# Batch 0's q of the first chunk loaded in 2-KB rows and turned by products with a 64-column selector

## The chip, the core and the metric

The kernel runs on one core of a Trainium2 chip. The metric is the device time of one execution in microseconds (us), the median over several runs. Engines: TensorE (PE, with its weight loads as PEld), VectorE (DVE), ScalarE (ACT), GpSimd (POOL), and SyncE (SP), which only issues DMAs.

## What is computed

Attention with a decay per head in blocks of 64 tokens, for 4 batches, 8 heads, 768 tokens and head dimension 64, and behind it a two-layer network with 512 inputs and 2048 hidden units. All inputs and the output are fp32.

```
for b in range(S // 64):
    qb, kb, vb = q[:, :, sl], k[:, :, sl], v[:, :, sl]
    intra = (qb @ kb.T * Dmask) @ vb              # Dmask[i, j] = lam**(i-j) for i >= j, else 0
    inter = (qb * lam**(pos+1)) @ kv_state
    out[:, :, sl] = intra + inter
    kv_state = lam**64 * kv_state + (kb * lam**(63-pos)).T @ vb
x = out, as (4*768, 512)
h = x @ w_in
g = h + sin(alpha*h)**2 / alpha
result = g @ w_out
```

## The kernel before

**Chunks.** The tokens go in six chunks of 128 per batch (`T = 128`, `NT = 6`); one chunk of all four batches makes a group of 512 tokens for the network. The code is written out by hand in the order in which each engine shall run it (`manual_schedule`): each engine executes its own instructions in that order, and semaphores join them. While the network of group g runs (`hidden`, `project`), the attention of the next chunk is woven in between.

**First chunk.** It has its own path, since nothing runs beside it. Per batch: k and q are turned so that the head dimension lies on partitions (`turn`, `turn_in_two`, `turn_rows_begin` and `turn_rows_end`), `scores1` makes the scores of all eight heads in two PSUM banks and VectorE multiplies them by the mask table `C0` into `STm` (L356), and `outs` multiplies by v and brings the result, for all but batch 0 with the factor table `Etab` (L370), into `xt`, the input of `hidden`. In batch 0 the factor lam**(i+1) is already in q, so `outs(0, 0, 6, A)` copies without a factor.

**Loads.** k and q of batch 0 come as fp32 through SP's hardware queue (`raw_k`, `raw_q`, L81), in rows of one token and head (64 numbers, 256 bytes); everything else comes through GpSimd's software queue, in this order: k and q of batches 1 to 3 (L104, L114), v of all batches (L104, L125), `w_in` in five pieces (L89), `w_out`'s first block (L92), and then the next chunk. GpSimd's loads convert to bf16 on the way.

**Rows of eight tokens.** q of batches 1 to 3 is loaded by `load_q_rows` with eight tokens of one head on one partition (2 KB a row), partition p holding head p % 8 and tokens 8 (p // 8) to 8 (p // 8) + 7. `turn_rows` turns this with sixteen products per batch: for each of the eight places e in a row, and each half of the heads, 64 columns of q against 64 columns of `by_head`, a permuted identity. They write fp32 in PSUM; L314 copies to `QKT`.

**Batch 0's q.** `raw_q` has one token per partition and all heads. VectorE multiplies it by `Rq` (128 x 8: factor by token and head, an exponential on ScalarE at L179 of `lnlam` with the column `pcol[:, 1]`) into bf16 (L578). `turn_in_two` makes four 128 x 128 transposes (L295), and ScalarE and VectorE copy half each (L296, L297).

**Small tables.** GpSimd's iota makes `dist` (column less partition). From it VectorE makes `iden`, the columns of `pcol` (L149), the triangle `tri` (L155), `tri64` (two 64 x 64 copies, L158, read only by the `mask_table` of the later chunks), `pos_row` (L163), `idf` (L164) and, once `lnlam` is there, `ln_x` (L186) and `by_head` (L188). `spin` puts products on TensorE whose result nobody reads.

Of the kernel before, what the change touches and what calls it, by code (L numbers as in the profile page):

```python
# [15 lines left out]
def kernel(  # L16
# [11 lines left out]
    nc = tc.nc  # L28
    P = nc.NUM_PARTITIONS

    B, H, S, D = q.shape
    T = 128
    NT = S // T
    HP = H // 2
# [23 lines left out]
    def bank(nm, n, dtype=FP32):  # L58
        return psum.tile([P, 512 if dtype is FP32 else 1024], dtype, name=nm, tag=f"b{n}")
# [16 lines left out]
            d[t] = p.tile([P, B, H, D], BF16, name=nm)  # L76

    raw = {}
    for nm, eng in (("k0", nc.sync), ("q0", nc.sync)):
        raw[nm] = rawp.tile([P, H, D], FP32, name=f"raw_{nm}")  # L80
        eng.dma_start(out=raw[nm][:], in_=NAT[nm[0]][1][int(nm[1]), :, 0:T, :].rearrange("h p e -> p h e"))  # L81
# [23 lines left out]

    new_chunk(0)
    new_chunk(1)
    E8 = T * H // P

    def q_rows(b):  # L110
        return qn[0][:, b].rearrange("p h d -> p (h d)")

    def load_q_rows(b):
        nc.gpsimd.dma_start(out=q_rows(b), in_=q[b, :, 0:T, :].rearrange("h (n e) d -> n h (e d)", e=E8))  # L114
# [21 lines left out]
    def spin(n, bk, cols=256):  # L136
        ps = bank("hps", bk)
        for _ in range(n):
            nc.tensor.matmul(out=ps[:, 0:cols], lhsT=fill[:, 0:P], rhs=fill[:, 0:cols], start=True, stop=True)  # L139
# [3 lines left out]
    pcol = consts.tile([P, 5], FP32, name="pcol")  # L143
# [4 lines left out]
    def column(rows, n, factor, base):  # L148
        nc.vector.tensor_scalar(out=pcol[rows, n:n + 1], in0=dist[rows, 0:1], scalar1=factor, scalar2=base,  # L149
                                op0=ALU.mult, op1=ALU.add)  # L150
# [3 lines left out]
    column(ALL, 0, 1.0, -1.0)  # L154
    nc.vector.tensor_scalar(out=tri[:], in0=dist[:], scalar1=0.0, scalar2=None, op0=ALU.is_ge)  # L155
    tri64 = consts.tile([P, D], FP32, name="tri64")
    for half in HALF:
        nc.vector.tensor_copy(out=tri64[half, :], in_=tri[half, half])  # L158
    column(ALL, 2, 1.0, T - 1.0)
    for n, half in enumerate(HALF):  # L160
        column(half, 3, 1.0, n * D - 1.0)
        column(half, 4, 1.0, (n + 1) * D - 1.0)
    nc.vector.tensor_scalar(out=pos_row[:], in0=dist[:], scalar1=pcol[:, 1:2], scalar2=None, op0=ALU.add)  # L163
    nc.vector.tensor_scalar(out=idf[:], in0=dist[0:NFC, 0:NFC], scalar1=0.0, scalar2=None, op0=ALU.is_equal)  # L164
# [12 lines left out]
    def powers(nm, n, src, shape):  # L177
        t = consts.tile(shape, FP32, name=nm)
        nc.scalar.activation(out=t[:], in_=src, func=ACTF.Exp, scale=pcol[:, n:n + 1])  # L179
        return t  # L180

    Rq = powers("Rq", 1, lnlam[:, 0:H], [P, H])
    NE = powers("NE", 0, by_pair, [P, 2, HP])
    ln_x = consts.tile([P, NDC], FP32, name="ln_x")
    for hd, half in enumerate(HALF):
# [19 lines left out]
    def decay_of_pair(pr):  # L205
        for hd, half in enumerate(HALF):
            nc.scalar.activation(out=L64[half, pr, :], in_=lnlam[half, pr + hd:pr + hd + H - 1:2],
                                 func=ACTF.Exp, scale=float(D))
# [80 lines left out]
        else:  # L289
            nc.scalar.copy(out=both[t][:, :, b, :, :], in_=ps)  # L290

    def turn_in_two(t, b, n):
        ps = bank("T_ps", n, BF16)[:].rearrange("p (n c i) -> p n c i", n=2, c=HP)[:, 1]
        for hp in range(HP):
            nc.tensor.transpose(out=ps[:, hp, :], in_=qn[t][:, b, 2 * hp:2 * hp + 2, :], identity=iden[:])  # L295
        nc.scalar.copy(out=both[t][:, 1, b, 0:2, :], in_=ps[:, 0:2])  # L296
        nc.vector.tensor_copy(out=both[t][:, 1, b, 2:4, :], in_=ps[:, 2:4])  # L297

    rows_ps = {}

    def turn_rows(b, es):
# [276 lines left out]
    nc.vector.tensor_tensor(out=qn[0][:, 0, :, :], in0=raw["q0"][:], op=ALU.mult,  # L578
                            in1=Rq[:].unsqueeze(2).broadcast_to([P, H, D]))
# [234 lines left out]
```

## Time and profile before

| what | value |
|---|---|
| median of 3 runs | 207.41 us (207.37 to 207.46) |
| the profiled execution | 207.33 us |
| its span, from the first instruction to the last | 205.6 us |
| granted TensorE clock, mean | 0.999 |
| TensorE busy | 198.1 us, 96% of the span |
| VectorE, ScalarE, GpSimd busy | 131.5, 143.2 and 106.5 us |
| software DMA queue | 74528 packets, 13.37 MB |

The span is what the profile's times refer to, from 0; the 1.7 us between span and time lie around it. A row of the timeline gives start, length, engine, line, operation, what is written from what, its shape, how many were merged into the row, and in brackets the idle time of the engine before it with what ended it. A stretch of the windows view gives for each engine busy time and number of instructions, then the granted clock, the mean load of the 16 DMA engines and the GB/s that they moved (bytes written).

### The profile page before, as it was taken

What the parts mean: (1) busy time and instruction counts of PE and PEld (TensorE: products, weight loads), DVE (VectorE), ACT (ScalarE), POOL (GpSimd) and SP (SyncE); (2) the same over time, 40 slices, a digit from 0 to 9 for tenths busy, and PEclk for the clock granted to TensorE, in tenths of its full rate; (3) what the DMA queues carried; (4) which work ended last, traced back from release to release, by engine and by line L of the source; (5) the groups of instructions that cost most, each with busy time, mean ns of one, the idle gap of its engine ahead of it and who ended that gap; (6) DMA issues with size and microseconds to landing.
All of it is one profiled execution on the core that took longest, in us unless ns stands there. A gap on an engine that the chain in (4) does not pass through costs nothing.

```text
span 205.6 us, 5385 instructions
## 1 busy us (share of the span) xinstructions
PE 198.1 (96%) x2235; PEld 98.3 (48%) x2265; DVE 131.5 (64%) x219; ACT 143.2 (70%) x241; POOL 106.5 (52%) x112
## 2 busy tenths in 40 slices
PE   7999989999999999999999999999999999999994
PEld 2764445554454444445444445444445444444443
DVE  7794979473889878967556967555967544444000
ACT  7798987224999799676776666776666787887121
POOL 8999939988979975999966930002000000000000
PEclk9999999999999999999999999999999999999999
DMA  8999999999989999899999929401101101110213
GB/s 132 170 178 205 203 162 176 189 176 154 150 275 105 128 151 184 82 150 155 152 149 155 181 64 192 117 3 51 54 0 54 51 0 54 53 51 0 104 51 105
DMA packets 96683, 24.49 MB, mean 119 GB/s; under 512 B 87938, under 2 KB 94226, under 8 KB 96658
## 3 DMA queue, kind: packets, MB, share of 16 engines
q0 software_dynamic: 74528, 13.37, 86.9%
q1 hardware_dynamic: 22128, 10.76, 25.5%
q8 instruction: 18, 0.29, 0.6%
q14 instruction: 7, 0.06, 0.1%
q10 hardware_dynamic: 2, 0.00, 0.0%
HBM read 27.27 MB, written 6.29 MB: 163 GB/s over the span
## 4 chain that ended last, share of the span: by engine, by line
PE 84%; DMA 7%; POOL 6%; issue 1%; ACT 1%; POOLq 0%; ACTq 0%
PE ops L535 39%; PE hps L507 35%; DMA w_out<-in_moe_w_out_dram 7%; PE O_ps L457 2%; POOL w_in L89 2%; PE hps L560 2%; PE F_ps L443 2%; PE KV_ps L423 2%; POOL kn L104 1%; PE O_ps L482 1%; POOL vn L104 1%; PE T_ps L338 1%; POOL qn L114 1%; POOL vn L125 1%; ACT QKT L344 1%
## 5 line engine op out<-in xcount | busy, mean ns | idle before, releaser
L524 DVE SCALAR_TENSOR_TENSOR gall<-s,r_sb,hps 128x512 bf16<-128x512 bf16 x96 | 71.1, 745 | 44.5 <-ACT s L515 44.3
L507 PE MATMUL hps<-xt,w_in 128*128 128x512 bf16 x369 | 94.3, 379 | 1.1 <-issue 0.3
L535 PE MATMUL ops<-w_out,gall 128*128 128x512 bf16 x353 | 90.4, 380 | 1.7 <-DMA w_out<-in_moe_w_out_dram 0.6
L510 ACT ACTIVATE s_sb<-hps,alpha_sb 128x512 bf16<-128x512 f32 x96 | 65.2, 684 | 32.0 <-PE hps L507 31.5
L515 ACT ACTIVATE s<-s_sb 128x512 bf16<-128x512 bf16 x91 | 57.3, 630 | 2.8
L507 PEld LDWEIGHTS <-w_in 128*128 128x128 bf16 x384 | 36.6, 98 | 42.8 <-DMA w_in<-in_moe_w_in_dram 0.3
L535 PEld LDWEIGHTS <-gall 128*128 128x128 bf16 x368 | 34.6, 98 | 41.5 <-DMA w_out<-in_moe_w_out_dram 1.1
L257 POOL TENSOR_TENSOR kdec<-kn,R 128x1024 bf16<-128x1024 bf16 x12 | 22.9, 1937 | 4.2 <-DMA kn<-in_k_dram 4.1
L392 POOL CAST sb<-S 128x512 bf16<-128x512 f32 x20 | 12.3, 621 | 21.3 <-DVE S L399 21.3
L388 POOL TENSOR_TENSOR SD<-S,L 128x512 f32<-128x512 f32 x16 | 16.8, 1050 | 8.6 <-DVE S L399 8.5
L489 DVE TENSOR_TENSOR xt<-O_ps,Etab 128x512 bf16<-128x512 f32 x20 | 12.8, 684 | 6.4 <-PE O_ps L482 6.4
L104 POOL DMA_DIRECT2D vn<-in_v_dram x13 | 14.7, 1137 | 0.0
L542 DVE COPY o_sb<-ops 128x512 f32<-128x512 f32 x15 | 10.3, 689 | 4.2 <-PE ops L535 4.2
L450 DVE TENSOR_TENSOR STm<-F_ps,C 128x512 bf16<-128x512 f32 x20 | 12.8, 683 | 0.3 <-PE F_ps L443 0.3
L544 ACT COPY o_sb<-ops 128x512 f32<-128x512 f32 x8 | 4.6, 576 | 12.0 <-PE ops L535 12.0
L399 DVE TENSOR_TENSOR S<-SD,KV_ps 128x512 f32<-128x512 f32 x16 | 10.8, 683 | 0.1
L104 POOL DMA_DIRECT2D kn<-in_k_dram x9 | 10.0, 1113 | 0.4 <-issue 0.3
L344 ACT COPY QKT<-T_ps 128x512 bf16<-128x512 bf16 x8 | 4.3, 586 | 5.3 <-PE T_ps L341 5.3
L139 PE MATMUL hps<-fill 128*128 128x256 bf16 (+1 forms) x24 | 6.5, 391 | 1.4 <-DVE fill L132 1.4
L104 POOL DMA_DIRECT2D qn<-in_q_dram x6 | 7.1, 1188 | 0.0
L457 PEld LDWEIGHTS <-sb 64*64 64x64 bf16 x320 | 4.3, 108 | 4.8 <-issue 4.7
L356 DVE TENSOR_TENSOR STm<-F_ps,C 128x512 bf16<-128x512 f32 x8 | 5.2, 686 | 0.8 <-PE F_ps L352 0.4
(92 smaller groups left out, 116.8 us busy)
## 6 DMA issues: line engine op xcount, KB each, us to landing
out_dram<-o_sb SPq DMA_DIRECT2D x19, 256.0 KB, 2.4
vn<-in_v_dram POOLq DMA_DIRECT2D x10, 256.0 KB, 7.9
w_out<-in_moe_w_out_dram POOLq DMA_DIRECT2D x4, 512.0 KB, 10.8
w_in<-in_moe_w_in_dram POOLq DMA_DIRECT2D x3, 512.0 KB, 9.4
kn<-in_k_dram POOLq DMA_DIRECT2D x6, 256.0 KB, 8.7
qn<-in_q_dram POOLq DMA_DIRECT2D x6, 256.0 KB, 8.5
out_dram<-o_sb SPq DMA_DIRECT2D x8, 128.0 KB, 1.8
kn<-in_k_dram POOLq DMA_DIRECT2D x4, 240.0 KB, 6.7
```

The source lines that it names most:

```text
L104: nc.gpsimd.dma_start(out=to, in_=by_head)
L257: nc.gpsimd.tensor_tensor(out=kdec[t][:, b0:b1, :, :], in0=kn[t][:, b0:b1, :, :], in1=R[:, o:o + H].unsqueeze(1).unsqueeze(3).broadcast_to ...
L388: nc.gpsimd.tensor_tensor(out=pair(SD, pr), in0=pair(S_of[n], pr), op=ALU.mult, in1=L64[:, pr].unsqueeze(1).unsqueeze(3).broadcast_to([P, ...
L392: nc.gpsimd.tensor_copy(out=pair(dst, pr), in_=pair(S_of[n], pr))
L399: nc.vector.tensor_tensor(out=S, in0=pair(SD, pr), in1=ps, op=ALU.add)
L450: nc.vector.tensor_tensor(out=st[:, hd], in0=att["F", t, pr, hd], op=ALU.mult, in1=of_mask(C64, t, pr, hd).unsqueeze(1).broadcast_to([P, 2 ...
L489: nc.vector.tensor_tensor(out=xview(t)[:, 2 * pr:2 * pr + 2, blk, :, :], in0=att["O", t, pr, blk], in1=Eb, op=ALU.mult)
L507: nc.tensor.matmul(out=hps[:], lhsT=w[:, c, (f % 4) * P:(f % 4 + 1) * P], rhs=xt[g][:, c, :], start=(c == 0), stop=(c == NDC - 1))
L510: nc.scalar.activation(out=s_sb[:], in_=hps[:], func=ACTF.Sin, scale=alpha_sb[:, f:f + 1])
L515: nc.scalar.activation(out=s2[:], in_=s_sb[:], func=ACTF.Square)
L524: nc.vector.scalar_tensor_tensor(out=gall[g][:, f, :], in0=s2[:], scalar=r_sb[:, f:f + 1], in1=hps[:], op0=ALU.mult, op1=ALU.add)
L535: nc.tensor.matmul(out=ops[:], lhsT=gall[g][:, f, m * P:(m + 1) * P], rhs=w_out_sb[part][:, f % 4, :], start=(f == 0), stop=(f == NFC - 1))
```

## The change

Batch 0's q is loaded in the same rows of eight tokens as the other batches, still as fp32 through SP's queue. Its factor is therefore no longer by token (partition) and head (column), but by head and token group (partition) and place in the row (column): `Rq` is now the exponential of `pos8`, the token's number plus one, scaled by a column `ln_row` that holds the logarithm of the partition's own head. To make these, seven small VectorE operations are new: `of_head` (which head a partition has, a sum over `iden`), `by_number`, two columns of `pcol`, `pos8`, `ln_h` and `ln_row`. The product with `Rq` goes ahead of the first mask table. Batch 0 is turned by sixteen products like the others, `turn_in_two` is dropped, and the two copies by halves now read fp32. The two fill products (`spin(2, 3)`) are dropped. The first half of batch 1's row products goes behind batch 0's scores. The copies into `tri64` go behind the reciprocal of alpha at the end of the first chunk, and `idf` and the five later columns behind `ln_row`.

```diff
-    for nm, eng in (("k0", nc.sync), ("q0", nc.sync)):
-        raw[nm] = rawp.tile([P, H, D], FP32, name=f"raw_{nm}")
-        eng.dma_start(out=raw[nm][:], in_=NAT[nm[0]][1][int(nm[1]), :, 0:T, :].rearrange("h p e -> p h e"))
+    E8 = T * H // P
+    def rows_of_eight(b):
+        return q[b, :, 0:T, :].rearrange("h (n e) d -> n h (e d)", e=E8)
+    raw["k0"] = rawp.tile([P, H, D], FP32, name="raw_k0")
+    raw["q0"] = rawp.tile([P, E8, D], FP32, name="raw_q0")
+    nc.sync.dma_start(out=raw["k0"][:], in_=k[0, :, 0:T, :].rearrange("h p e -> p h e"))
+    nc.sync.dma_start(out=raw["q0"][:].rearrange("p e d -> p (e d)"), in_=rows_of_eight(0))
...
-    for half in HALF:
-        nc.vector.tensor_copy(out=tri64[half, :], in_=tri[half, half])
-    column(ALL, 2, 1.0, T - 1.0)
-    for n, half in enumerate(HALF):
-        column(half, 3, 1.0, n * D - 1.0)
-        column(half, 4, 1.0, (n + 1) * D - 1.0)
     nc.vector.tensor_scalar(out=pos_row[:], in0=dist[:], scalar1=pcol[:, 1:2], scalar2=None, op0=ALU.add)
-    nc.vector.tensor_scalar(out=idf[:], in0=dist[0:NFC, 0:NFC], scalar1=0.0, scalar2=None, op0=ALU.is_equal)
...
+    nc.vector.tensor_reduce(out=of_head[:], in_=iden[:].rearrange("p (n h) -> p h n", h=H), axis=AX, op=ALU.add)
+    nc.vector.tensor_tensor(out=by_number[:], in0=of_head[:], in1=pos_row[:, 0:H], op=ALU.mult)
+    nc.vector.tensor_reduce(out=pcol[:, 5:6], in_=by_number[:], axis=AX, op=ALU.add)
+    nc.vector.scalar_tensor_tensor(out=pcol[:, 6:7], in0=pcol[:, 5:6], scalar=-1.0, in1=dist[:, 0:1],
+                                   op0=ALU.mult, op1=ALU.subtract)
+    nc.vector.tensor_scalar(out=pos8[:], in0=pos_row[:, 0:E8], scalar1=pcol[:, 6:7], scalar2=1.0,
+                            op0=ALU.add, op1=ALU.add)
...
-    Rq = powers("Rq", 1, lnlam[:, 0:H], [P, H])
+    nc.vector.tensor_tensor(out=ln_h[:], in0=lnlam[:, 0:H], in1=of_head[:], op=ALU.mult)
+    nc.vector.tensor_reduce(out=ln_row[:], in_=ln_h[:], axis=AX, op=ALU.add)
+    column(ALL, 2, 1.0, T - 1.0)
+    for n, half in enumerate(HALF):
+        column(half, 3, 1.0, n * D - 1.0)
+        column(half, 4, 1.0, (n + 1) * D - 1.0)
+    nc.vector.tensor_scalar(out=idf[:], in0=dist[0:NFC, 0:NFC], scalar1=0.0, scalar2=None, op0=ALU.is_equal)
+    nc.scalar.activation(out=Rq[:], in_=pos8[:], func=ACTF.Exp, scale=ln_row[:, 0:1])
...
-    def turn_rows_end(b):
+    def turn_rows_end(b, shared=False):
         turn_rows(b, range(E8 // 2, E8))
-        nc.scalar.copy(out=both[0][:, 1, b, :, :], in_=rows_ps.pop(b).rearrange("p (c i) -> p c i", c=HP))
+        ps = rows_ps.pop(b).rearrange("p (c i) -> p c i", c=HP)
+        if shared:
+            nc.scalar.copy(out=both[0][:, 1, b, 0:2, :], in_=ps[:, 0:2])
+            nc.vector.tensor_copy(out=both[0][:, 1, b, 2:4, :], in_=ps[:, 2:4])
+        else:
+            nc.scalar.copy(out=both[0][:, 1, b, :, :], in_=ps)
...
+    nc.vector.tensor_tensor(out=qn[0][:, 0, :, :], in0=raw["q0"][:], op=ALU.mult,
+                            in1=Rq[:].unsqueeze(2).broadcast_to([P, E8, D]))
     mask_128(0)
-    nc.vector.tensor_tensor(out=qn[0][:, 0, :, :], in0=raw["q0"][:], op=ALU.mult,
-                            in1=Rq[:].unsqueeze(2).broadcast_to([P, H, D]))
     mask_128(1)
     decay_64()
     turn(0, "k", 0, 4, A)
-    spin(2, 3)
-    turn_in_two(0, 0, 5)
+    turn_rows_begin(0, 5)
+    turn_rows_end(0, True)
     turn(0, "k", 1, 1, A)
     decay_of_pair(0)
+    scores1(0, 0, (6, 7))
     turn_rows_begin(1, 2)
-    scores1(0, 0, (6, 7))
     turn_rows_end(1)
...
     nc.vector.reciprocal(out=r_sb[:], in_=alpha_sb[:])
+    for half in HALF:
+        nc.vector.tensor_copy(out=tri64[half, :], in_=tri[half, half])
     spin(3, 3)
     load_w_out(0)
```

More of the change, by code (lines that the diff above doesn't have):

```diff
@@ L107 @@
     new_chunk(1)
-    E8 = T * H // P
     def q_rows(b):
@@ L113, in load_q_rows @@
     def load_q_rows(b):
-        nc.gpsimd.dma_start(out=q_rows(b), in_=q[b, :, 0:T, :].rearrange("h (n e) d -> n h (e d)", e=E8))
+        nc.gpsimd.dma_start(out=q_rows(b), in_=rows_of_eight(b))
     dist = consts.tile([P, T], FP32, name="dist")
@@ L142 @@
     nc.vector.tensor_scalar(out=iden[:], in0=dist[:], scalar1=0.0, scalar2=None, op0=ALU.is_equal)
-    pcol = consts.tile([P, 5], FP32, name="pcol")
+    pcol = consts.tile([P, 7], FP32, name="pcol")
     tri = consts.tile([P, T], FP32, name="tri")
@@ L156 @@
     tri64 = consts.tile([P, D], FP32, name="tri64")
-    for half in HALF:
-        nc.vector.tensor_copy(out=tri64[half, :], in_=tri[half, half])
-    column(ALL, 2, 1.0, T - 1.0)
-    for n, half in enumerate(HALF):
-        column(half, 3, 1.0, n * D - 1.0)
-        column(half, 4, 1.0, (n + 1) * D - 1.0)
-    nc.vector.tensor_scalar(out=pos_row[:], in0=dist[:], scalar1=pcol[:, 1:2], scalar2=None, op0=ALU.add)
-    nc.vector.tensor_scalar(out=idf[:], in0=dist[0:NFC, 0:NFC], scalar1=0.0, scalar2=None, op0=ALU.is_equal)
+    nc.vector.tensor_scalar(out=pos_row[:], in0=dist[:], scalar1=pcol[:, 1:2], scalar2=None, op0=ALU.add)
+    of_head = consts.tile([P, H], FP32, name="of_head")
+    by_number = consts.tile([P, H], FP32, name="by_number")
+    pos8 = consts.tile([P, E8], FP32, name="pos8")
+    AX = mybir.AxisListType.X
+    nc.vector.tensor_reduce(out=of_head[:], in_=iden[:].rearrange("p (n h) -> p h n", h=H), axis=AX, op=ALU.add)
[5 more added lines that the diff above has]
+                            op0=ALU.add, op1=ALU.add)
     SB = [consts.tile([P, B, HP, D], BF16, name=f"sb{n}") for n in range(3)]
@@ L180, in powers @@
         return t
-    Rq = powers("Rq", 1, lnlam[:, 0:H], [P, H])
+    ln_h = consts.tile([P, H], FP32, name="ln_h")
+    ln_row = consts.tile([P, 1], FP32, name="ln_row")
+    nc.vector.tensor_tensor(out=ln_h[:], in0=lnlam[:, 0:H], in1=of_head[:], op=ALU.mult)
[5 more added lines that the diff above has]
+    nc.vector.tensor_scalar(out=idf[:], in0=dist[0:NFC, 0:NFC], scalar1=0.0, scalar2=None, op0=ALU.is_equal)
+    Rq = consts.tile([P, E8], FP32, name="Rq")
+    nc.scalar.activation(out=Rq[:], in_=pos8[:], func=ACTF.Exp, scale=ln_row[:, 0:1])
     NE = powers("NE", 0, by_pair, [P, 2, HP])
@@ L290, in turns @@
             nc.scalar.copy(out=both[t][:, :, b, :, :], in_=ps)
[L292 to L297, printed above, removed]
     rows_ps = {}
```

## The prediction

> **What bounds the kernel now.** I read the page's first part, then the chain that ended last, then the waits behind the first 17 us, and then the first 30 us by timeline.
>
> ```profile
> span 205.6 us, 5385 instructions
> PE 198.1 (96%) x2235; PEld 98.3 (48%) x2265; DVE 131.5 (64%) x219; ACT 143.2 (70%) x241; POOL 106.5 (52%) x112
> ```
>
> TensorE is busy for 96% of the span, so a change in the first 8 us counts only if it removes idle TensorE time later on. Where that idle time is, the chain (start, length, what) and the timeline show:
>
> ```profile
> 9.91 3.59 POOL w_in L89 x5
> 13.50 13.73 DMA w_out<-in_moe_w_out_dram
> ...
> 27.28 1.04 PE L535 MATMUL ops<-w_out,gall 128*128 128x512 bf16 x4 [0.63 <-DMA w_out<-in_moe_w_out_dram]
> 29.22 0.69 ACT L510 ACTIVATE s_sb<-hps,alpha_sb 128x512 bf16<-128x512 f32 x1 [0.60 <-PE hps L507]
> ```
>
> The reader is to see one wait. TensorE has nothing to do from 26.65 to 27.28, because the first block of w_out, issued at 13.50, has landed at 27.23 only. Behind it the chain is TensorE work. So two times decide: when w_out lands, and when TensorE gets there (26.65 now, 0.63 to spare). A gain passes to the end as long as ScalarE has room too; it idles 0.60 at 29.22, so about 0.6 can pass.
>
> w_out lands so late because the DMA engines never pause (half-microsecond windows; the last column is GB/s moved):
>
> ```profile
> 4.00:4.50 0.50, 0.50 (x2) 0.15 (x1) 0.41 (x2) 0.49 (x3) 0.50 (x2) 1.00 1.95 163
> 11.50:12.00 0.50, 0.42 (x10) 0.31 (x8) 0.50 (x1) 0.47 (x3) 0.50 (x1) 1.00 2.38 153
> 18.50:19.00 0.50, 0.50 (x4) 0.25 (x3) 0.50 (x2) 0.50 (x2) 0.50 (x1) 1.00 1.22 203
> ```
>
> The short rows of k and v move at about 155 GB/s, weights at 203. All of it stands in one software queue, and ahead of that queue stand raw k and raw q. Whatever these two give back, w_out should get. The DMA view of three stretches (2 to 4 us; 2.9 to 3.8, where raw rows of 256 B move; 132.0 to 132.5, where a store of 2-KB rows moves), and the landings:
>
> ```profile
> q1 hardware_dynamic: 1893, 0.48, 109.4%
> q0 software_dynamic: 18, 0.00, 1.8%
> ...
> DMA packets 960, 0.24 MB, mean 269 GB/s; under 512 B 960, under 2 KB 960, under 8 KB 960
> ...
> DMA packets 94, 0.19 MB, mean 385 GB/s; under 512 B 0, under 2 KB 0, under 8 KB 94
> ...
> raw_k<-in_k_dram SPq DMA_DIRECT2D x1, 256.0 KB, 3.3
> raw_q<-in_q_dram SPq DMA_DIRECT2D x1, 256.0 KB, 4.0
> ```
>
> **Part 1, the load of q0.** It goes from 1024 pieces of 256 B to 128 of 2 KB, still 256 KB. At the short rows' rate, 0.262 MB / 269 GB/s is 0.97 us; at the store's rate, 0.262 / 385 is 0.68. So 0.29 is the lower bound of what the engines give back; a loss is excluded by the windows, where long rows never move slower than short ones. Upper bound: raw k lands at 0.73 + 3.3 = 4.03 and raw q at 1.25 + 4.0 = 5.25 (issues below), 1.22 apart on the engine that is last; 0.68 in its place gives 0.54. w_out's landing is also set by the last engine, so I take a value near the upper row, 0.45. It passes on if the software queue can start earlier: only 18 of its packets went before 4 us, although its first issue was done at 1.33 + 1.08 = 2.41. That queue was waiting for the engines, not for GpSimd, as far as the rows show. [...]
>
> w_out then lands at 27.23 - 0.45 = 26.78, and its first product can start at 26.83.
>
> **Part 2, the road of q0 to the first scores.**
>
> ```profile
> 1.25 0.56 SPq L81 DMA_DIRECT2D raw_q<-in_q_dram  x1
> 1.33 1.08 POOL L104 DMA_DIRECT2D kn<-in_k_dram  x1 [0.27 <-issue]
> 1.45 0.61 PE L139 MATMUL hps<-fill 128*128 128x512 bf16 x1 [1.45 <-DVE fill L132]
> 1.65 0.20 DVE L155 TENSOR_SCALAR tri<-dist 128x128 f32<-128x128 f32 x1
> 1.89 0.72 DVE L158 COPY tri<-tri 64x64 f32<-64x64 f32 x2
> 2.64 0.49 DVE L149 TENSOR_SCALAR pcol<-dist 128x1 f32<-128x1 f32 x5
> 2.82 1.28 ACT L179 ACT_TABLE_LOAD   x1
> 2.94 0.90 POOL L104 DMA_DIRECT2D kn<-in_k_dram  x1
> 3.16 0.73 DVE L163 TENSOR_SCALAR pos_row<-dist,pcol 128x128 f32<-128x128 f32 x1
> 3.36 0.54 DVE L164 TENSOR_SCALAR idf<-dist 16x16 f32<-16x16 f32 x1
> 3.82 0.32 DVE L186 COPY ln_x<-lnlam 64x4 f32<-64x4 f32 x2
> 4.17 0.27 DVE L188 COPY by_head<-iden 128x128 bf16<-128x128 bf16 x1
> 5.26 0.61 PE L320 MATMUL T_ps<-iden,kn 128*128 128x128 bf16 x4
> 5.28 0.69 DVE L578 TENSOR_TENSOR qn<-raw_q,Rq 128x512 bf16<-128x512 f32 x1
> 6.09 0.64 PE L295 MATMUL T_ps<-iden,qn 128*128 128x128 bf16 x4
> 6.52 0.64 PE L320 MATMUL T_ps<-iden,kn 128*128 128x128 bf16 x4
> 6.76 0.37 ACT L296 COPY QKT<-T_ps 128x256 bf16<-128x256 bf16 x1 [0.27 <-PE T_ps L295]
> 7.17 0.29 DVE L297 COPY QKT<-T_ps 128x256 bf16<-128x256 bf16 x1 [0.59 <-ACT QKT L296]
> 7.79 0.42 PE L305 MATMUL T_ps<-by_head,qn 128*64 128x64 bf16 x8
> 7.89 5.54 DVE L356 TENSOR_TENSOR STm<-F_ps,C 128x512 bf16<-128x512 f32 x8 [0.43 <-PE F_ps L352]
> 8.13 0.40 PE L320 MATMUL T_ps<-iden,kn 128*128 128x128 bf16 x4
> ```
>
> VectorE: gone ahead of q0's product are the two tri64 copies (0.72) and the first mask (5.28 - 4.64 = 0.64, now behind it). New are seven small operations, each reading the one before: at the 0.15 of L149's kind and a gap of 0.03 some 0.18 each, 1.3 in all (lower bound; the upper one is the third rival). pos_row moves up and ends between 2.05 and 2.6, ln_row thus at 3.4 to 3.9. The exponential Rq could not start before its table load ends at 4.10 anyway, so the chain is hidden there with 0.2 to 0.7 to spare. The other small tables follow: columns 0.49, idf 0.20 (L155's, when nothing stalls), ln_x 0.32, by_head 0.27, together 1.28; they end at 4.7 to 5.2. Raw q lands at 5.25 - 0.45 = 4.80. The product starts at about 4.95 in place of 5.28 and ends at 5.65.
>
> TensorE: k0's transposes still wait for the cast and start at 5.26. The four transposes of q0 and two fill products go, sixteen 64-column products come at 5.67. Eight take 0.42 at L305, of which some 0.25 is the latency of one; sixteen take 0.59 at that pace. But early TensorE runs at half pace (the same four transposes take 0.64 at 6.52 and 0.40 at 8.13), which makes it up to 0.95. q0 stands in PSUM at 6.3 to 6.65, before at 6.73. The copy by halves stays in series: 0.37 on ScalarE, then 0.29 on VectorE, now out of fp32, for which I take 0.42 (bounds 0.29 and the 0.69 of L356's 512 columns). First masked scores: 7.6 to 8.0 against 7.89, so about no change.
>
> Moved: the first half of batch 1's row products stood before the scores of batch 0, under the wait for those copies; now all sixteen stand behind, so q of batch 1 is some 0.2 later, and scores of batch 1 with it. From there VectorE's eight products follow each other nearly without a gap (5.54, or 1.39 per batch), so the delay stays. I take +0.13 for the whole stage, bounds -0.1 and +0.3. Who waits for that:
>
> ```profile
> 13.34 2.02 DVE L370 TENSOR_TENSOR xt<-O_ps,Etab 128x512 bf16<-128x512 f32 x4
> 14.26 3.88 POOL L257 TENSOR_TENSOR kdec<-kn,R 128x1024 bf16<-128x1024 bf16 x2
> 15.15 1.42 PEld L507 LDWEIGHTS <-w_in 128*128 128x128 bf16 x8 [0.32 <-DMA w_in<-in_moe_w_in_dram]
> 17.68 0.75 DVE L524 SCALAR_TENSOR_TENSOR gall<-s,r_sb,hps 128x512 bf16<-128x512 bf16 x1 [2.16 <-ACT s L515]
> ```
>
> The first hidden product started when w_in landed; with that earlier, the last xt products of L370 are what is late next. TensorE then comes to the w_out wait at 26.65 + 0.13 = 26.78, before 26.83. The tri64 copies, now behind the reciprocal, run under VectorE's pause of 2.16 ahead of 17.68, which hides them. If GpSimd's decay products of 14.26 to 18.14 hold both up to their end, the first gall product starts at 18.14 + 0.4, 0.8 late; TensorE has eight PSUM banks for hidden products before it needs one back, so I cost that at nothing too. Without those banks it would be the 0.8 less the 0.63 to spare, 0.2.
>
> **Sum.** First w_out product at 26.83 for 27.28: -0.45, against the profiled execution 207.33 - 0.45 = 206.88; the median of the runs stands 0.08 above it, so 207.41 - 0.45 = 206.96. This case's own range is 206.75 to 207.1 (0.3 to 0.65 gained). What a measurement of this kernel can tell from no change is about 0.2%, 0.41 us.
>
> **Rivals.** *The transfer was hidden anyway.* If raw q's end does not start the software queue earlier, because the queue starts 1.5 us after its issue for reasons of its own, w_out lands at 27.23 as now: 207.4. For it: 18 packets went before 4 us, none early. Against it: queue 1 kept all engines busy until just then.
>
> *TensorE's pace is late to double* (slower). The doubling came between 6.5 and 8.1 after unbroken work from 1.45, partly fill products; two of them go. If q0 is late, TensorE stands still from 5.67, and if such a pause starts the count anew, 5.6 us more go at half pace, to about 11.3. The 4.2 us of dense work from 7.1 then make only half their way: +2.1, TensorE at the wait at 28.75, end +1.5: 208.9. It decides once the pause is long enough; I expect one near 0. [...] The granted clock in the windows shows 1.00 throughout, so only the rows' pace can tell.
>
> *The small operations get stuck* (slower). L163 and L164 end together at 3.9, as GpSimd's k issue ends (3.84), and take 0.73 and 0.54 where L155, of L163's shape, takes 0.20. If the seven take 0.35 to 0.52 each, ln_row comes at 4.85 to 6.0, and ScalarE, in order, holds k0's cast behind Rq: 0.75 to 1.9 late, with the 0.13 past the spare 0.63 by 0.25 to 1.4: 207.7 to 208.8. It decides from ln_row at about 4.6. [...]
>
> **Numbers.** My case has 0.56 (0.45 beyond 0.41 us, 0.11 within), the hidden transfer 0.20 (0.17 within, 0.03 a little slower by the order of batch 1), the late pace 0.12, the stuck operations 0.12 (0.02 within). Faster 0.45, same 0.30, slower 0.25. The range 206.7 to 208.0 leaves out the late pace and the worse half of the stuck operations, under 0.2.
>
> **What would show it.** Right: raw_q lands near 4.8; q0's product starts before 5; w_out lands near 26.8 and the wait of L535 shrinks from 0.63 to under 0.2; the first STm stays near 7.9. Wrong: raw_q lands earlier but w_out does not; or L535 starts without a DMA wait and later than 26.9, the road of q0 being longer; or transposes at 8.1 still take 0.64.

## The result, and the profile after

The changed kernel takes 208.91 us (median of 22 runs, 207.99 to 210.52), the kernel before 207.62 beside it (207.27 to 209.1). The ratio is 1.0057, with a 95% interval of 1.0041 to 1.0073: slower, by more than the 0.2% that a measurement can tell. The profiled execution took 207.99 us, the lowest of the 22, 0.66 more than the profiled one before (207.33). So two things are to be explained: 0.66 that is there even in the quickest execution, and some 0.6 more in the median.

The page's first part:

```profile
span 206.2 us, 5412 instructions
PE 197.9 (96%) x2245; PEld 98.2 (48%) x2275; DVE 134.3 (65%) x226; ACT 143.0 (69%) x241; POOL 106.7 (52%) x112
```

TensorE does no more work than before (197.9 us for 198.1) in ten more products and ten more weight loads: the time went into pauses. The timeline of the first chunk:

```profile
5.43 0.50 PE L336 MATMUL T_ps<-iden,kn 128*128 128x128 bf16 x4
5.68 0.69 DVE L593 TENSOR_TENSOR qn<-raw_q,Rq 128x512 bf16<-128x512 f32 x1 [0.84 <-ACT NE L187]
6.43 0.64 PE L316 MATMUL T_ps<-by_head,qn 128*64 128x64 bf16 x16 [0.50 <-DVE qn L593]
...
7.11 0.37 ACT L327 CAST QKT<-T_ps 128x256 bf16<-128x256 f32 x1 [0.56 <-PE T_ps L316]
...
7.51 0.42 DVE L328 CAST QKT<-T_ps 128x256 bf16<-128x256 f32 x1
...
8.21 0.64 PE L316 MATMUL T_ps<-by_head,qn 128*64 128x64 bf16 x16
8.30 1.29 DVE L372 TENSOR_TENSOR STm<-F_ps,C 128x512 bf16<-128x512 f32 x2 [0.36 <-PE F_ps L368]
...
8.78 0.40 PE L336 MATMUL T_ps<-iden,kn 128*128 128x128 bf16 x4
```

VectorE was through with the small tables at 4.85 and stood idle for 0.84; q's product started at 5.68 (before: 5.28). The row puts the wait down to ScalarE's NE, the last of which also ended at 5.58; but the chain of waits has the landing of raw q there, and in kernels 6 and 7 below, too, the product starts 0.10 after that landing (5.78 and 5.88, 5.48 and 5.58). What came last is raw q. The first masked scores come at 8.30 (7.89), the transposes of batch 2's k at 8.78 (8.13): 0.41 and 0.65 late. The DMA view shows why the first is. Raw q landed at 1.24 + 4.3, to the hundredth at 5.58, in place of 5.26; here are the landings, and the stretch from 3.3 to 3.9 us, in which 2-KB rows move:

```profile
DMA packets 80, 0.16 MB, mean 266 GB/s; under 512 B 2, under 2 KB 2, under 8 KB 80
...
raw_k<-in_k_dram SPq DMA_DIRECT2D x1, 256.0 KB, 3.3
raw_q<-in_q_dram SPq DMA_DIRECT2D x1, 256.0 KB, 4.3
```

The same stretch of the kernel before, in rows of 256 B:

```profile
DMA packets 645, 0.16 MB, mean 273 GB/s; under 512 B 645, under 2 KB 645, under 8 KB 645
```

An eighth of the pieces, and the same rate. Packet by packet the trace says more. The median packet of 2 KB took 0.084 us on its engine, just what the packets of the store at 132 us take (median 0.084); but 21 of the 128 took 0.15 to 0.75, together 7.5 of the 17.1 us that all packets of raw q add up to. In rows of 256 B every packet of raw k took 0.015 to 0.018.

At the first block of w_out the waiting is over all the same, 0.14 earlier than before, since w_out landed at 26.84 for 27.23 (timeline):

```profile
26.26 1.04 PE L523 MATMUL hps<-xt,w_in 128*128 128x512 bf16 x4
27.14 1.03 PE L551 MATMUL ops<-w_out,gall 128*128 128x512 bf16 x4
```

Matched product by product, TensorE is 0.15 ahead of the kernel before from 27.3 to 40.3 us, and from 42.8 on 0.61 behind (0.67 at the end). The chain of waits shows what lies between:

```profile
39.08 0.97 PE ops L551 x4
40.05 0.14 PE O_ps L473
40.20 0.25 PE O_ps L498 x32
40.45 0.26 PE KV_ps L439 x28
40.71 0.59 issue
41.30 0.22 PE KV_ps L439 x2
41.51 0.16 issue
```

In the middle of a row of products of one line, TensorE stands for 0.6 us and waits for no semaphore ("issue"). The kernel before has only the second pause of 0.16 there:

```profile
40.60 0.30 PE KV_ps L423 x30
40.90 0.16 issue
```

Nothing in the change touches these products; what is new is that 20 more TensorE instructions stand ahead of them. The DMA queues between 38.5 and 40.1 us show a packet of instructions:

```profile
q8 instruction: 1, 0.02, 3.5%
```

It starts at 38.96 and takes 0.89, 16 KB; in the kernel before there is one like it at 39.00.

### The profile page after: what moved, and what is told of

It reads as the page before. It is cut to its first block, busy times and chain, and to the rows that moved or that the text cites. A ratio compares the mean times of both kernels' runs of the same rounds, so it can differ in the third digit from the quotient of the medians.

```text
span 206.2 us, 5412 instructions
## 1 busy us (share of the span) xinstructions
PE 197.9 (96%) x2245; PEld 98.2 (48%) x2275; DVE 134.3 (65%) x226; ACT 143.0 (69%) x241; POOL 106.7 (52%) x112
## 4 chain that ended last, share of the span: by engine, by line
PE 76%; POOL 8%; DMA 5%; issue 4%; ACT 3%; DVE 1%; SPq 0%; POOLq 0%; ACTq 0%; DVEq 0%
PE hps L523 32%; PE ops L551 32%; DMA vn<-in_v_dram 3%; DMA raw_q<-in_q_dram 2%; POOL SD L404 2%; ACT s_sb L526 2%; PE O_ps L473 2%; PE hps L576 2%; PE F_ps L459 1%; PE KV_ps L439 1%; POOL vn L110 1%; PE O_ps L498 1%; POOL sb L408 1%; PE T_ps L316 1%; POOL kdec L275 1%
## 5 line engine op out<-in xcount | busy, mean ns | idle before, releaser
L523 PEld LDWEIGHTS <-w_in 128*128 128x128 bf16 x384 | 36.6, 98 | 42.8 <-issue 0.5
L143 PE MATMUL hps<-fill 128*128 128x256 bf16 (+1 forms) x22 | 5.9, 387 | 1.5 <-DVE fill L136 1.5
## 6 DMA issues: line engine op xcount, KB each, us to landing
w_out<-in_moe_w_out_dram POOLq DMA_DIRECT2D x4, 512.0 KB, 10.7
```

What stands on the lines that cost most here:

```text
L523: nc.tensor.matmul(out=hps[:], lhsT=w[:, c, (f % 4) * P:(f % 4 + 1) * P], rhs=xt[g][:, c, :], start=(c == 0), stop=(c == NDC - 1))
```

## The experiments

The expectations name theories by letters. Of the pause at 40.7: A, TensorE runs out of instructions, since 20 more of them bring the end of a block into a dense stretch; B, something lands late or GpSimd is late. Of the first chunk: C, the masks hold up q's copy; D, raw q's landing and the series of steps behind it. Later ones are E to S, told in the texts. Each is a change of a few lines to the changed kernel, unless it says otherwise.

**1. Twenty TensorE instructions fewer.** In the five fill groups between 9 and 16 us:

```
-    spin(3, 1)            (twice)      +    spin(1, 1, 512)
-    spin(3, 3)            (3 times)    +    spin(1, 3, 512)
```

> The changed kernel with the five groups of three 256-column fill products (ahead of and between the outs of the first chunk) as one 512-column fill each: 20 PE instructions fewer, so that every instruction behind them has the number that it has in the kernel before. Theory A (the 0.77 us gap of TensorE inside the KV products of L439 at 40.5 is TensorE out of instructions: the 20 instructions that the change adds move the end of a loaded block into this dense stretch): the gap is gone, the time falls by 0.6 to 0.8 us against the changed kernel, to about -0.1 us against the kernel before. Theory B (the gap is a late transfer or a late GpSimd product): the gap stays, the time stays 0.5 to 1.2 us over the kernel before.

Measured: 208.53 (207.87 to 210.51), ratio 1.0058 [1.0033, 1.0084], which is no gain on the changed kernel's 1.0057, where A expected 0.6 to 0.8 us. But the pause at 40.7 is gone, as A has it (timeline):

```profile
41.40 0.49 PE L439 MATMUL KV_ps<-vn,kdec 64*64 64x64 bf16 x32
41.81 1.04 PE L551 MATMUL ops<-w_out,gall 128*128 128x512 bf16 x4
```

What hid the gain in this execution is that its first chunk ran late, by up to 1.9 us, and the windows say why (column PEclk, the granted clock, the third from the right):

```profile
8.00:9.00 1.00, 1.00 (x20) 0.84 (x19) 0.74 (x2) 0.29 (x2) 1.00 (x2) 0.64 1.88 168
9.00:10.00 1.00, 1.00 (x16) 0.69 (x12) 0.55 (x1) 0.78 (x2) 1.00 (x3) 0.50 2.02 161
10.00:11.00 1.00, 1.00 (x20) 0.63 (x18) 0.14 (x1) 0.35 (x1) 1.00 (x2) 0.50 2.43 155
11.00:12.00 1.00, 1.00 (x20) 0.69 (x16) 1.00 (x2) 0.56 (x2) 1.00 (x2) 0.66 2.42 154
```

The clock was granted in full at 4.86, taken back at 8.27 and granted again at 11.69: 3.4 us at half pace, after a stretch in which TensorE had stood still ahead of q's turning (0.71) and of the scores (0.17). That is the second theme of this case.

**2. The kernel before with twenty more.** In the same five groups:

```
-    spin(3, 1)            (twice)      +    spin(5, 1, 154)
-    spin(3, 3)            (3 times)    +    spin(5, 3, 154)
```

> The kernel before with the same five groups as five 154-column fills each (770 columns for 768): 20 PE instructions more, nothing else. Theory A: a gap of 0.5 to 0.8 us appears in the KV products near 40.5 and the time rises by 0.5 to 0.8 us. Theory B: no gap, the time within 0.1 us of the kernel before.

Measured: 208.10 (207.76 to 208.41), kernel before 207.56; the ratio, 1.0009 [0.9985, 1.0033], doesn't tell them apart (A expected 0.5 to 0.8 us more), the traces do. The pause appears in a kernel that has nothing else of the change:

```profile
40.36 0.45 PE L423 MATMUL KV_ps<-vn,kdec 64*64 64x64 bf16 x30
41.43 0.22 PE L423 MATMUL KV_ps<-vn,kdec 64*64 64x64 bf16 x2 [0.63 <-issue]
41.58 1.04 PE L535 MATMUL ops<-w_out,gall 128*128 128x512 bf16 x4
```

Up to it TensorE is 0.05 ahead of the kernel before, behind it 0.75 late, to the end. With run 1 this speaks for A, and nothing for B; the count under 9 to 11 settles it.

**3. The first mask ahead of q's product again.**

```
+    mask_128(0)
     nc.vector.tensor_tensor(out=qn[0][:, 0, :, :], in0=raw["q0"][:], op=ALU.mult, ...)
-    mask_128(0)
```

> The changed kernel with the first mask table ahead of q's product again, as before. Theory C (the two masks behind q's product hold up VectorE's half of the copy of q): first masked scores 0.3 us earlier, and as much of the time. Theory D (raw q's landing at 5.58 and the series of product, sixteen turns and two copies set it): VectorE's idle 0.84 us takes the mask, the first masked scores move by under 0.1 us, and so does the time.

Measured: 209.05 (208.05 to 210.66), ratio 1.0079 [1.0054, 1.0103]. Products from 10.7 us on are 1.05 late in place of 0.65, but in this execution raw q landed at 6.06, 0.48 later. From that landing to the first masked scores (8.70) it was 2.64, in the changed kernel 2.72: 0.08 less, where C expected 0.3 and D under 0.1. C falls: the order of the masks is not what costs.

**4. Batch 1's first row products ahead of batch 0's scores again.**

```
+    turn_rows_begin(1, 2)
     scores1(0, 0, (6, 7))
-    turn_rows_begin(1, 2)
```

> The changed kernel with the first half of batch 1's row products back ahead of batch 0's scores. If their new place makes the second 0.24 us of the 0.65 by which the first chunk is late, the scores of batch 1 come 0.2 us earlier and the first hidden product at 15.6 for 15.8. By theory A the time hardly moves all the same, as TensorE then waits 0.2 longer for instructions at 40.5; by theory B it falls by 0.2.

Measured: 209.13 (207.93 to 209.44), ratio 1.0063 [1.004, 1.0087]. Nothing to be read on the order: in the profiled execution the products kept half pace until 11.0 (sixteen turning products 1.06 us for 0.64) and the first chunk was 1.87 late. It is tried again in 7, with the fills back.

**5. The two dropped fill products back** (theory E).

```
     turn(0, "k", 0, 4, A)
+    spin(2, 3)
     turn_rows_begin(0, 5)
```

> The changed kernel with the two dropped fill products put back at their old place, between the transposes of batch 0's k and the turning of its q. Theory E (without the fills TensorE stands still 0.4 to 0.9 us ahead of q's turning; in some executions that falls into the window by which the granted clock is raised, the clock then comes 3.4 us or more later and the first chunk runs longer at half pace; this spreads the times from 208.0 to 210.5): full pace from about 7 us in the profile as before the change, lowest time within 0.3 of the changed kernel's lowest, the highest under 208.8, median 208.0 to 208.3. Theory F (the spread comes from elsewhere, such as late transfers): spread and median as in the changed kernel, some 208 to 210.5 around 208.9. The instruction stall at 40.5 us stays under both.

Measured: 208.38 (208.13 to 209.3), ratio 1.0035 [1.0019, 1.0051]. The median falls by 0.53, the lowest time does not. Two of 12 executions, for 14 of 22, lie more than 0.7 above the lowest. E's other signs are weaker: the highest is not under 208.8, and in the profile full pace came at 7.93, so that the sixteen turning products took 1.06 us and the first chunk was 1.03 late.

**6. Fills back, and 20 instructions fewer** (5 and 1 together).

> As the kernel before it, and the later fill groups of three products cut to one each, which takes 20 instructions out of TensorE's stream again. Theory A (the 0.6 to 0.8 us stall in the dense products at 40.5 us comes from the number of instructions ahead of it) with E: no stall at 40.5, 0.6 to 0.8 less than with the fills alone, median 207.3 to 207.6, thus level with the kernel before the change. If only A held and not E: lowest about 207.3, median above 208.

Measured: 207.92 (207.42 to 210.54), ratio 1.0017 [1.0001, 1.0033]: another 0.46, less than the 0.6 to 0.8 expected. With only the fills back the pause had measured 0.34 by the shift of the products behind it, not 0.76.

**7. The same, and rows first** (6 and 4 together).

> As the kernel before it, and batch 1's first eight row products ahead of batch 0's scores again. Theory D1 (0.24 of the 0.65 by which the first chunk is late is the order of batch 1): transposes of batch 2's k 0.2 earlier than in the kernel before it, first w_out product 0.2 earlier, median 207.1 to 207.4. Rival (VectorE's eight mask products set the pace and the order costs nothing): the same within 0.1.

Measured: 207.57 (207.25 to 208.89), kernel before 207.51, ratio 1.0000 [0.9984, 1.0016]. It carries the load in long rows, the factor table, the sixteen products and the moved tables, and is level, though not at the 207.1 to 207.4 that D1 expected. From the first masked scores to the transposes of batch 2's k it is 0.25 us in its profile (8.20 and 8.45), in the changed kernel 0.48, before 0.24: the order of batch 1 is worth 0.23 there. Timeline of its profile:

```profile
27.42 1.04 PE L551 MATMUL ops<-w_out,gall 128*128 128x512 bf16 x4 [0.36 <-DMA w_out<-in_moe_w_out_dram]
...
40.56 0.49 PE L439 MATMUL KV_ps<-vn,kdec 64*64 64x64 bf16 x32
40.98 1.04 PE L551 MATMUL ops<-w_out,gall 128*128 128x512 bf16 x4
```

No pause at 40.7, and the wait for w_out is back.

**8. The same, and q issued ahead of k.**

> As the kernel before it, and q of batch 0 issued ahead of its k on the hardware queue. Theory D2 (the late landing of raw q, 5.58 for 5.25, starts the road of q late): raw q lands near 4.1, its product starts at 4.9 when VectorE is through with the small tables; raw k lands at 5.4 to 5.6 and its cast is late by 0.8, its copy by 0.5 or more, so the first scores wait for k now: first masked scores 7.7 to 8.1, median within 0.3 of the kernel before it. If the 2-KB rows as such were what lands late: raw q still past 4.5 although it is first.

Measured: 208.81 (207.62 to 209.6), ratio 1.0052 [1.0029, 1.0075].

```profile
4.76 0.68 DVE L593 TENSOR_TENSOR qn<-raw_q,Rq 128x512 bf16<-128x512 f32 x1
...
6.41 0.40 PE L336 MATMUL T_ps<-iden,kn 128*128 128x128 bf16 x4 [1.15 <-ACT kn L587]
```

Raw q landed at 4.58, where raw k in rows of 256 B, when first, had landed at 4.0; q's product started at 4.76, as expected. But k came late, TensorE stood for 1.15, and nine of 12 executions lie more than 0.7 above the lowest; the median is 1.24 above kernel 7, not within 0.3. The DMA view of 2.2 to 3.05 us has only 171 GB/s in long rows:

```profile
DMA  9992999999200002090020209990999499449774
...
DMA packets 71, 0.15 MB, mean 171 GB/s; under 512 B 0, under 2 KB 0, under 8 KB 71
```

The zeros are not idle engines: the row counts a packet whole in the slice where it starts, and the packets of this stretch took 93% of the 16 engines' time. Twenty of the 128 packets took 0.17 to 0.69 us each, the median again 0.084. All 128 were through at 3.67, before the software queue's first packet at 4.20.

**9 to 11. The count of instructions, with fills back and rows first.** Kernel 7 has 20 instructions fewer than the first here, which has the five groups as they were, `spin(3, ...)`; the second has `spin(5, ..., 154)`, 40 more than kernel 7; the third has none of the five groups, 10 fewer than kernel 7.

> The changed kernel with the two fill products back and batch 1's first row products ahead of batch 0's scores, the later fill groups left as they are: 20 TensorE instructions more than in the best kernel so far (207.57). Theory A2 (the instruction packet for the block ahead of 40.5 us starts near 39.0 whatever the count, and its instructions run 2.3 us after that; TensorE, 20 instructions nearer to the block's end, gets there first): a stall of 0.3 to 0.7 at 40.7 to 41.4 is back. Theory G (an instruction packet of 16 KB between the last block of w_in and the first of w_out makes w_out 0.7 later; here it goes before 24 us): w_out lands 2.5 to 2.7 after the last of w_in, at 26.6 to 26.9, and TensorE waits less than 0.1 for it. Both together: 207.5 to 207.9. If G were wrong: w_out near 27.3, 207.9 to 208.3.

> As the kernel before it, but five products in place of three in each of the five later fill groups: 40 TensorE instructions more than in the best kernel so far. Theory A2 leaves two ways: if the block's packet starts earlier by a stretch of dense products (before 38.4), no stall, 207.2 to 207.5; if it stays at 39.0, the stall is 0.6 to 1.0, 207.8 to 208.2. By G w_out lands without the 0.7.

> As the best kernel so far (fills back, rows first), but with the five later fill groups gone altogether: 10 TensorE instructions fewer than there. Theory G: the packet that went at 25.21 goes after 26 now, w_out lands 2.5 to 2.7 after the last of w_in and the wait of 0.36 for it goes: 207.1 to 207.4, below the kernel before the change. Theory A2: no stall at 40.5. Against it: with the fills of 9 to 16 us gone, the granted clock may fall back in some executions: then times up to 210.

Measured: 208.49 (207.76 to 209.53), 208.39 (208.19 to 208.92), 208.68 (207.49 to 209.01), each above the range of its theories. Timelines of the first:

```profile
27.07 1.03 PE L551 MATMUL ops<-w_out,gall 128*128 128x512 bf16 x4
...
41.11 0.22 PE L439 MATMUL KV_ps<-vn,kdec 64*64 64x64 bf16 x4 [0.49 <-issue]
```

and of the second:

```profile
41.71 0.31 PE L439 MATMUL KV_ps<-vn,kdec 64*64 64x64 bf16 x14 [0.57 <-issue]
```

The place of the pause in the row is seen to move: 2 products of 32 are left behind the pause in the changed kernel, 4 with 4 instructions more, 14 with 24 more (a product and its load are two instructions). The packet starts at 38.67 and 39.23, and the pause ends 2.4 to 2.5 us later; in the changed kernel 2.34, in run 2 2.27. Over all profiles the pause stands at one place of the stream: 477 weight loads lie ahead of it in each of the seven that have it (the changed kernel and runs 2 to 5, 9 and 10), and the 478th comes 2.27 to 2.48 us after the packet, which starts between 38.67 and 39.84 in them. In the ten without it TensorE gets to the 478th load 2.74 us or more after the packet. So theory A2 holds: the packet's start (38.67 to 40.01 over all 17) hardly follows the count, and the price is the time by which TensorE gets to that load too early. The second kernel has another such pause, worth 0.26, near 47.4, 2.2 after a packet at 45.20.

In the third no pause is left at 40.7, but without the fills the clock fell back in eight executions of 12 (timeline and window of the profiled one):

```profile
15.56 0.59 PE L523 MATMUL hps<-xt,w_in 128*128 128x512 bf16 x1 [1.24 <-DVE xt L386]
```

```profile
15.60:18.90 3.30, 3.08 (x7) 0.95 (x8) 2.89 (x4) 1.83 (x4) 3.17 (x3) 0.50 1.25 206
```

The eight took 208.55 to 209.01 (mean clock 0.991 or 0.992), the other four 207.49 to 207.94; the 207.1 to 207.4 hoped for came in none.

**12. The kernel before, without its two fill products.**

> The kernel before the change, without its two fill products ahead of q's transposes. Theory E (what spreads the changed kernel's times is TensorE standing still ahead of q's turning, long enough to miss a window of the clock): here the pause is 0.2 to 0.4 us, against 0.5 to 0.9 in the changed kernel and 1.15 with q issued first, so a few executions of twelve (2 to 5) come out over 208.3, the rest at 207.3 to 207.8 as before. If the fills alone mattered, whatever the pause: as many as in the changed kernel, half or more. If neither: as before.

Measured: 207.58 (207.08 to 208.68), kernel before 207.56: the same, with one of 12 executions over 208.3, fewer than the two to five expected. It was the profiled one, where one DMA engine brought its part of raw q only at 6.37:

```profile
7.14 0.40 PE L295 MATMUL T_ps<-iden,qn 128*128 128x128 bf16 x4 [1.48 <-DVE qn L578]
```

TensorE stood for 1.48, the clock was taken back from 8.29 to 11.70, and the end is 1.12 late. So the two products as such aren't needed: eleven of 12 executions do without them. That q came in time in those, and left no pause to fill, is inferred; the one trace is of the late execution.

**13 and 14. Why raw q lands late.** Kernel 7 with q in two loads of 1-KB rows, and kernel 7 with a memset of 1024 columns on GpSimd ahead of its first load:

```
-    nc.sync.dma_start(out=raw["q0"][:].rearrange("p e d -> p (e d)"), in_=rows_of_eight(0))
+    for e in range(2):
+        nc.sync.dma_start(out=raw["q0"][:, 4 * e:4 * e + 4, :].rearrange("p e d -> p (e d)"),
+                          in_=rows_of_eight(0)[:, :, 256 * e:256 * e + 256])
```

```
+    hold = consts.tile([P, 1024], FP32, name="hold")
+    nc.gpsimd.memset(hold[:], 0.0)
     for b in range(1, B):
```

> The best kernel so far (fills back, fewer later fills, rows first: 207.57), with q of batch 0 in two loads of 1-KB rows, four tokens each, in place of one of 2-KB rows. Theory R (the long rows as such land late, because the last engines still hold 2-KB pieces when the software queue comes in): raw q lands at 5.2 to 5.4 in place of 5.48 to 5.78, q's product starts 0.2 earlier, median 207.3 to 207.6. Theory S (the software queue's start alone sets it, whatever the rows): raw q lands at 5.5 to 5.8 again, median 207.5 to 207.9; the second issue of 0.56 costs nothing under either.

> The best kernel so far, with a memset of 1024 columns on GpSimd ahead of its first load, so that the software queue starts about 1 us later; its landings, w_out's too, are then about 1 later, and the time is no test of anything. Theory S: without packets of the software queue beside it raw q lands at 4.8 to 5.2. Theory R, and the other way that the hardware queue itself is slow with these rows: raw q at 5.4 to 5.8 again.

Measured: 208.94 (208.45 to 209.75), ratio 1.0067 [1.0042, 1.0092], and one execution of 208.38. In the first, raw q landed at 4.92 and 6.12, one half each; the software queue's first packet came in between, at 3.38 (3.61 in kernel 7), and VectorE waited:

```profile
6.25 0.69 DVE L595 TENSOR_TENSOR qn<-raw_q,Rq 128x512 bf16<-128x512 f32 x1 [1.43 <-DMA raw_q<-in_q_dram]
```

Theory R falls in this form: two loads landed later than one. In the second the software queue came in hardly later: its first issue was done at 2.99 for 2.41, but its first packet went at 3.97 for 3.89 in the changed kernel (3.61 in kernel 7), and raw q landed at 5.31. That run doesn't tell R from S.

**15. The kernel before with twenty fewer instructions** (as in 1), to move the instruction packet away from w_out.

> The kernel before the change, with one product of 512 columns in place of three of 256 in each of the five later fill groups: 20 TensorE instructions fewer. Theory G (an instruction packet between w_in's last block and w_out's first makes w_out 0.7 late; in the kernel before it goes at 25.07): the packet goes after 26 here, w_out lands at 26.4 to 26.7 in place of 27.23, TensorE waits less than 0.1 for it in place of 0.63: 206.9 to 207.2, so faster than both kernels. If G were wrong: w_out at 27.2 again and 207.4 to 207.6. If the thinner fills let the granted clock fall back as without any: some times over 208.3.

Measured: 207.69 (206.97 to 208.67), ratio 0.9995 [0.9967, 1.0024]. Its lowest time is the lowest of all, and three of 12 lie over 208.3; the 206.9 to 207.2 expected was not reached in the median. In the profiled execution the packet went at 25.73, still between the last block of w_in (23.94) and w_out, which landed at 27.98. Over all profiles: w_out landed 2.21 to 2.69 after the last of w_in in the eight where no packet of instructions lies between, and 2.50 to 4.04 in the nine where one does (five of them 3.2 to 3.4). Two pairs of kernels that differ in the later fill groups alone agree: the kernel before and run 2 with 3.25 and 2.50, kernels 7 and 9 with 3.34 and 2.21, each time with the packet between in the first. So G holds in its direction, not with a fixed 0.7: three of the nine landed as early as without a packet.

## Why the prediction was wrong

Three steps of the sum failed. The gain from the load of q0 (0.45) was not there. The road of q0 (+0.13) was late by 0.65. And the place of twenty more TensorE instructions in the stream, for which the sum has no term, cost 0.76. In the profiled execution they add up so: the first w_out product came at 27.14 for the forecast 26.83, so -0.45 became -0.14; with the 0.76 at 40.7 that is +0.62, of the 0.66 measured.

**The load of q0: wrong, and the step on which the forecast gain rested.** It took a gain of 0.45 with 0.29 as the lower bound, and excluded a loss. Raw q landed 0.32 later. The rate of 385 GB/s was that of a store at 132 us; the load moved at 266 GB/s, against 273 in short rows. The rate was right for most packets (median 0.084 us, as in the store); what was left out is that a sixth of them take 2 to 9 times as long (0.15 to 0.75). With these, all packets of raw q add up to 17.1 us, for 18.3 us for the same 256 KB of raw k in short rows in the same profile: 0.07 us on each of 16 engines. In the other profiles the 128 long packets behind k add up to 14.9 to 18.9. Over the profiles, raw q in 2-KB rows behind k landed at 5.31 to 6.06 (eleven), in rows of 256 B at 5.19, 5.26 and 5.30, and once at 6.37. In the changed kernel 14 of the 16 engines reported by 5.14, the last two at 5.49 and 5.58. That long rows are the cheaper ones isn't seen in the load as a whole; it is seen in most packets, since 2 KB keep an engine 0.084 us in one packet (the median) and 0.12 in eight (273 GB/s over 16 engines).

**"The software queue starts earlier": wrong.** It started at 3.89 for 3.86, and its loads landed some 0.3 later (the last of w_in 24.33 for 23.98). The reading behind it, that the queue waits for the engines, agrees with 13, where a gap between the two loads of q brought the start forward to 3.38, and a fixed 1.5 us after the issue (the first rival) does not: it was 0.98 in 13 and 14, 1.79 in 8. But the long rows kept the engines nearly as long as the short ones (17.1 us for 18.3), so there was no room to give.

**"w_out lands at 26.78, and its wait goes": came true, for another reason.** 26.84, and no wait. But the loads ahead of it were later, not earlier; what was gone is the packet of instructions between, at 23.74 in place of 25.07, which the twenty instructions had moved (run 2, the kernel before with twenty more, has it at 23.07). Kernel 7, with the same load, has it at 25.21 and waits again. That the forecast time of w_out came true is luck. The gain was 0.14, not 0.45, since TensorE came at 27.14.

**The road of q0, +0.13 (bounds -0.1 and +0.3): mis-sized, +0.65.** The seven small operations were hidden, as said. Some 0.4 came with raw q (product at 5.68, before at 5.28, forecast 4.95), the rest with batch 1's order, forecast as 0.2: 0.24 in the trace, and putting that order back in kernel 7 took 0.23 off there and 0.35 off the median, though the intervals of 6 and 7 overlap. And 0.65 is a lucky value: in this execution full pace came at 5.68, ahead of the turning products, in the kernel before at 7.19, in run 5 at 7.93 with the first chunk 1.03 late. The copy by halves took 0.37 and 0.42, as said.

**The twenty extra instructions: not in the sum.** They were costed by their run time alone. In the profiled execution their place in the stream cost 0.76, more than its whole loss of 0.66. That TensorE's instructions come in blocks, one to a packet, is theory A's reading. What the runs show of it: the packet ahead of w_out went at 25.07 in the kernel before, at 23.07 with twenty TensorE instructions more (run 2) and at 25.73 with twenty fewer (run 15), and the profile of the changed kernel has 18 packets of 16 KB and 4520 products and weight loads of TensorE, 251 to a packet.

**The tri64 copies, costed at nothing: right,** with a first gall product somewhat later than the 0.8 that was named.

```profile
16.09 2.61 DVE L637 COPY tri<-tri 64x64 f32<-64x64 f32 x2
18.73 0.75 DVE L540 SCALAR_TENSOR_TENSOR gall<-s,r_sb,hps 128x512 bf16<-128x512 bf16 x1
```

The first gall product came 1.05 later than before, and TensorE did not wait for it.

**The rivals.** *The transfer was hidden anyway* (0.20) was nearest to what the load did. *The small operations get stuck* did not happen.

*TensorE's pace is late to double* (0.12) is real: not in the changed kernel's profiled execution, whose full pace came at 5.68, but in those of runs 1 and 4. (The windows' granted clock of 1.00 from the start, which the prediction mentions, says nothing: run 4 shows 1.00 as well while its products run at half pace up to 11.0, since the record of the clock has no entry ahead of the first grant, in the kernel before none ahead of 7.19.) Its kind and its size were right (+1.9 in the first chunk, about +1.0 behind w_out, where it expected +2.1 and +1.5). The count that starts anew was not right: in run 1 the clock had been granted at 4.86 and was taken back, and it changed in steps of 3.4 us. And the pause was not "near 0": 0.35 to 0.95 in the profiles of 1, 3, 4 and the changed kernel itself.

It was wrong to give one answer for all executions, since the same kernel passes in some and fails in others; nor does the length of the pause alone decide, since 0.95 in run 3 and 1.15 in run 8 did not cost the clock in their profiles. The granted clock changed in steps of 3.41 us (runs 1 and 12), and its first grant came anywhere from 4.86 to 11.01 in the profiles; that it goes by windows, as E has it, is the author's reading of these times, and what sets them is not shown. With the fills back the median fell by 0.53, which is most of the 0.6 that the profiled execution does not show. Without the fills (the changed kernel, 1, 3, 4) 33 of 50 executions lie more than 0.7 above their kernel's lowest, with them (5, 6, 7, 9, 10) 15 of 55; 8, 11, 13 and 14, which change the loads or take out the later fills, are left out. So theory E is borne out as a tendency; that the clock is the cause in each late execution is not shown, since only one of each kernel has a trace. Kernel 9 has the fills and still spreads from 207.76 to 209.53.

What stays open is why a sixth of the long packets take so long. It is not the software queue: in the changed kernel all 21 of them started before its first packet (3.89), and in 8 all 128 packets were through before it (3.67 and 4.20).

## What to carry to other kernels

Take the price of a transfer from a row of the same direction, size and time in the trace: here most packets of the load ran at the store's pace (0.084 us), and the few that didn't (21 of 128, 0.15 to 0.75) took the gain away. Twenty instructions more on the busiest engine cost 0.76 here near 41 us, by their place in the stream: look in the chain for "issue" in a dense stretch of small products, compare the place of the pause in the stream with a kernel of another count, and try a few instructions more or fewer before a change is judged. Two fill products that cover a pause in the first microseconds took 0.53 off the median here (run 5), and where the start decides, one profiled execution is not the median (207.99 and 208.91).

## What was not expected of the hardware

- TensorE stood for 0.17 to 0.63 us without a semaphore near 41 us in seven profiles of 17, always behind the 477th weight load; from the start of the 16-KB packet to the first load behind the pause it was 2.27 to 2.48 us in them.
- That packet took 0.89 us in the changed kernel. In the kernel before one of 0.96 us (25.07) stood between the last block of w_in and w_out, and one of the 16 parts of w_out came late (fifteen by 26.48, the last at 27.23).
- Loads of 256 KB in 128 rows of 2 KB moved no faster than in 1024 rows of 256 B (266 and 273 GB/s), though the median packet ran at 0.084 us: 21 of 128 took 0.15 to 0.75. Issued first, with nothing beside them, 20 still took 0.17 to 0.69 (171 GB/s).
- Pauses of TensorE of 0.71 us (run 1) and 1.48 us (run 12) in the first 9 us went with a fall of the granted clock to half for 3.4 us; 0.95 (run 3) and 1.15 (run 8) did not.
